# Convolving two query parts at once, and moving staged q and k by DMA, in a fused attention and gated-convolution kernel

## Chip, cores and metric

The kernel runs on one core of one Trainium2 chip. The metric is the device time of one execution in microseconds. A profile is one execution, taken separately; its span (214.9 us before) runs from the first to the last instruction and is some 1.7 us shorter than the time of that same execution. Executions whose time is more than 1.5% above the fastest of the same kernel count as slow and enter no comparison.

## The reference

```python
scores = np.matmul(q, k.transpose(0, 1, 3, 2)) / np.sqrt(D)        # B=4, H=8, S=768, D=64
mask   = window of +-1 block of 32 | first and last block, row and column | 3 sampled blocks per row block
attn   = softmax(np.where(mask, scores, -1e9))
x      = (attn @ v).transpose(0, 2, 1, 3).reshape(B, S, H * D)     # 4 x 768 x 512

h = np.maximum(x @ w_in, 0.0)                                      # 4 x 768 x 1024
for k in range(3):                                                 # 3 taps along the sequence
    conv_out += conv_w[k] * hp[:, k:k + S, :]                      # hp: h padded by one row on each side
out = (h / (1 + np.exp(-conv_out))) @ w_out                        # 4 x 768 x 512
```

## The kernel before

The words used below:

- A **pair** P (0 to 15) is two heads of one batch, four pairs to a batch. From pair 6 on its q and k are loaded, transposed by DMA into a **staging tile** `tmp`, and copied from there into a **slot** (TensorE transposes the first six pairs): tile `et` (first head) and tile `ot` (second), whose last 24 rows carry the mask.
- A **half** n (0 to 7) is one query part of 384 rows of one batch, g = n mod 2. It is 18 **units**; a unit is eight score blocks (TensorE, into one of two `st` tiles), one exponential of 128 x 1024 (ScalarE, `pt<-st`) and eight value products (`av<-vt,pt`). I speak of the first to the eighth half and of batches 0 to 3.
- The **layers** of a half follow its attention: eight groups of first-layer products (`mix<-xT,winb`), a relu each (`hE<-mix`, on ScalarE or VectorE), then four **convolution steps** of two 128-channel chunks (multiplies `m<-hE,cw`, additions `m<-m`, tanh, tanh+1, gate `gT`), then three second-layer blocks (`mix<-woutb,gT`).
- The **planner**, part of the kernel, orders all instructions of all engines from modelled durations and latencies. The order is fixed when the program is built. Each engine, and each DMA queue, then works strictly in that order and waits where an input is late.

The staging, in the form of before: two transposes in the sync queue, two copies by VectorE.

```python
NSLOT = 6                                        # slots for q/k of a pair; two staging tiles
t0 = op({"SP": 1.3}, xp(0), ..., alloc=tb, lat=TLAT)                   # tmp <- q by DMA transpose
t1 = op({"SP": 1.3}, xp(1), ..., lat=TLAT)                             # tmp <- k
ce = op({"DVE": 0.5}, put(ET, 0),  due, [t0, t1, ...], alloc=slot_b[P], uses=[tb])
co = op({"DVE": 0.5}, put(OT, 64), due, [ce], uses=[slot_b[P], tb])
# put: copy_to(e, t[s][0:64], tmp_t[tb.index][r0:r0 + 64])
```

The convolution of one half, one step:

```python
hE_t = many(3, [128, NFFC, 640], BF16, "hE");  gT_t = many(4, [128, NFFC, 384], BF16, "gT")   # one half each
m_t  = many(3, [128, 2, 768], BF16, "m");      tn_t = many(3, [128, 768], BF16, "tn")
def mul(x, slot):                                 # tap x: two chunks of 384 columns
    for (o0, o1, src, w) in muls(x):
        nc.vector.tensor_scalar(out=m_t[cb.index][:, slot, o0:o1], in0=src, scalar1=w, scalar2=None, op0=ALU.mult)
m1 = op({"DVE": tm}, mul(1, 0), ...)              # centre tap
m0 = op({"DVE": tm}, mul(0, 1), ..., [edge])      # after GpSimd has copied the edge columns
ad1 = op({"DVE": t_d2(768)}, add, ...);  m2 = op(...mul(2, 1)...);  ad2 = op(...add...)
th = op({"ACT": 0.745}, ...Tanh, scale=0.5...)    # sigmoid(z) = (1 + tanh(z/2)) / 2
g1 = op(...tanh + 1...);  gate = op(...gT = (tanh + 1) * h / 2...)
# ... [cut: the one row that the two parts of a batch share is mended by p1, p2, p3]
```

The softmax here doesn't subtract the row's maximum and nothing guards it: scores larger than these inputs give would overflow.

Of the kernel before, what the change touches and what calls it, by code (L numbers as in the profile page):

```python
# [11 lines left out]
ALU = mybir.AluOpType  # L12
# [36 lines left out]
FLEX = 0.0345  # L49
# [4 lines left out]
class Scheduler:  # L54
# [108 lines left out]
    def backward(self, order):  # L163
# [34 lines left out]
        for o, t in zip(order, end):  # L198
            o.prio = -t
            o.outs = []  # L200
            for b in o.allocs:
                b.index = None
                b.pool.holders = []
# [10 lines left out]
def kernel(  # L214
# [21 lines left out]
    NSLOT = 6  # L236
# [22 lines left out]
    NTMP, NVN, NNAT, NPT, NXK, NXT, NHE, NCV, NGT, NOS = 2, 3, 3, 5, 3, 4, 3, 3, 4, 4  # L259
# [7 lines left out]
    hE_t = many(NHE, [128, NFFC, 640], BF16, "hE")  # L267
    m_t = many(NCV, [128, 2, 768], BF16, "m")
    tn_t = many(NCV, [128, 768], BF16, "tn")
    gT_t = many(NGT, [128, NFFC, 384], BF16, "gT")  # L270
# [48 lines left out]
    T0, PACE0, PACE1 = 8.0, 0.91, 1  # L319
    OFF = 32.0894  # L320
    XLAT, TLAT = 3.908, 9.2201
    S_FIRST, A_FIRST, R_FIRST, N_FIRST = 5.6663, -4, 0.1178, 0.842
    F1S, F2A, F2S = 0.03, 2.344, 0.191
    WO = 22.9467
    OFFL = 28
    PE_ = 0.0
    PASSES = 12
# [116 lines left out]
    def rows_to(dst, src):  # L444
        return lambda e: nc.sync.dma_start(out=dst[64:88], in_=src[64:88])

# [9 lines left out]
    for s in range(1, NSLOT):  # L456
        for t, m in ((ET, e_mask), (OT, o_mask)):
            if s == 1 and t is OT:
                m[s] = op({"POOL": 1.8}, pool_copy(t[s][64:88], t[0][64:88]), 2.5, [m[0]])
            elif s == 1:  # L460
                m[s] = op({"DVE": 0.58}, rows_by(t[s], t[0]), T(4.5 * s) - 2.5, [m[0]])
            else:
                m[s] = op({"SP": 0.46}, rows_to(t[s], t[0]), T(4.5 * s) - 6, [m[0]], lat=6.0,
                          earliest=T(18 + 2 * s) if s > 3 else 0.0)
# [4 lines left out]
    for s in range(NHE):  # L469
        def z(e, s=s):  # L470
            nc.vector.memset(hE_t[s][:, :, 639:640], 0.0)
        he_z[s] = op({"DVE": 0.15}, z, T(2))
# [24 lines left out]
    def qk_loads(P):  # L497
# [9 lines left out]
        k_iss[P] = ik  # L507
        return nb, lq, lk
# [41 lines left out]
    for P in range(NP):  # L550
# [23 lines left out]
        else:  # L574
# [12 lines left out]
            t0 = op({"SP": 1.3}, xp(0), due - 8, [lq], alloc=tb, uses=[nb], lat=TLAT)  # L587
            t1 = op({"SP": 1.3}, xp(1), due - 8, [lk], uses=[nb, tb], lat=TLAT)
            ce = op({"DVE": 0.5}, put(ET, 0), due, [t0, t1, slot_first.get(P - 1)], alloc=slot_b[P], uses=[tb])
            co = op({"DVE": 0.5}, put(OT, 64), due, [ce], uses=[slot_b[P], tb])  # L590
# [29 lines left out]
    def norm_ops(n, hp):  # L620
# [33 lines left out]
        xtr[(n, hp)] = op({"SP": 1.25}, tr, due - 5, [nm], lat=XLAT, uses=[xk] + us, alloc=al)  # L654
# [91 lines left out]
    def conv_gate(due, edge, relus, muls, gate_out, gate_h, heb, gtb, first_gt, last_tap=None):  # L746

        cb = Buf(P_cv)

        def mul(x, slot):  # L750
            def fn(e):
                for (o0, o1, src, w) in muls(x):
                    nc.vector.tensor_scalar(out=m_t[cb.index][:, slot, o0:o1], in0=src, scalar1=w, scalar2=None,  # L753
                                            op0=ALU.mult)
            return fn

        def add(e):
            m = m_t[cb.index]
            nc.vector.tensor_tensor(out=m[:, 0], in0=m[:, 0], in1=m[:, 1], op=ALU.add)  # L759
        nmul = len(edge[1])  # L760
        tm = sum(t_d4s(w_) for w_ in edge[1])
        m1 = op({"DVE": tm}, mul(1, 0), due + 1.7, list(relus) + [cw_op], alloc=cb, uses=[heb])
        m0 = op({"DVE": tm}, mul(0, 1), due + 2, [edge[0]], uses=[cb, heb])
        ad1 = op({"DVE": t_d2(768)}, add, due + 2.2, [m1, m0], uses=[cb])
        m2 = op({"DVE": tm}, mul(2, 1), due + 2.1, [edge[0], ad1], uses=[cb, heb])
        ad2 = op({"DVE": t_d2(768)}, add, due + 2.3, [ad1, m2], uses=[cb])
        if last_tap is not None:
            last_tap(cb, ad2, due)
        th = op({"ACT": 0.745}, lambda e: nc.scalar.activation(  # L769
            out=tn_t[cb.index], in_=m_t[cb.index][:, 0], func=AF.Tanh, bias=0.0, scale=0.5),  # L770
            due + 2.8 - R_FIRST, [ad2], uses=[cb])
        g1 = op({"DVE": t_d4(768)}, lambda e: nc.vector.tensor_scalar(  # L772
            out=tn_t[cb.index], in0=tn_t[cb.index], scalar1=1.0, scalar2=None, op0=ALU.add),
            due + 3.6, [th], uses=[cb])

        def gate(e):
            o, h = gate_out(), gate_h()
            t = tn_t[cb.index]
            if len(h.shape) == 3:
                t = t.rearrange("p (a b) -> p a b", a=2)  # L780
            nc.vector.tensor_tensor(out=o, in0=t, in1=h, op=ALU.mult)  # L781
        return op({"DVE": t_d2(768)}, gate, due + 3.7, [g1], uses=[cb, heb] + ([] if first_gt else [gtb]),
                  alloc=gtb if first_gt else None)

    def out_block(n, c, due, deps, parts=None):

        gb = gt_buf[n]
# [5 lines left out]
        for (mb, acc, take, o0, o1, on, by) in parts:  # L793
            ob = Buf(P_os)
            prev = None
            for a in range(4):
                def fn(e, a=a, acc=acc, o0=o0, o1=o1):
                    for ffc in (2 * a, 2 * a + 1):
                        nc.tensor.matmul(out=acc()[:, 0:o1 - o0], lhsT=gT_t[gb.index][:, ffc, 128 * c:128 * c + 128],  # L799
# [10 lines left out]
    heb_n, cvl_b, cvl_op, gates_n = {}, {}, {}, {}  # L810
    for n in range(NHALF):
        b, g = divmod(n, 2)
        lastn = n == NHALF - 1
        heb, gtb = Buf(P_he), Buf(P_gt)
        heb_n[n], gt_buf[n] = heb, gtb
        if g == 0:
            cvl_b[n] = Buf(P_cvl)
        relus, gates = [], []
        base = T(18 * (n + 1)) + (OFFL if lastn else OFF)
        for ffc in range(NFFC):  # L820
            due = base + W * F1S * ffc
            relus.append(ffn1(n, ffc, due, lambda ffc=ffc, heb=heb: hE_t[heb.index][:, ffc, 128:512], heb, ffc == 0))
            if ffc % 2 == 0:
                continue
            f0 = ffc - 1

            def edges(e, f0=f0, heb=heb, g=g, n=n):
                h = hE_t[heb.index]
                nc.gpsimd.tensor_copy(out=h[:, f0:f0 + 2, 1:128], in_=h[:, f0:f0 + 2, 384:511])  # L829
                nc.gpsimd.tensor_copy(out=h[:, f0:f0 + 2, 512:639], in_=h[:, f0:f0 + 2, 129:256])  # L830
                if g == 1:
                    nc.gpsimd.tensor_copy(out=h[:, f0:f0 + 2, 0:1],
                                          in_=hE_t[heb_n[n - 1].index][:, f0:f0 + 2, 511:512])
                else:
                    nc.gpsimd.memset(h[:, f0:f0 + 2, 0:1], 0.0)
            ed = op({"POOL": 1.0}, edges, due + 1.5, relus[f0:f0 + 2], uses=[heb] + ([heb_n[n - 1]] if g else []))

            def muls(x, f0=f0, heb=heb):
                return [(384 * y, 384 * y + 384, hE_t[heb.index][:, f0 + y, 128 * x:128 * x + 384],
                         cw[:, x, f0 + y:f0 + y + 1]) for y in range(2)]  # L840

            def save(cb, ad2, due, f0=f0, n=n):
                al = cvl_b[n] if f0 == 0 else None
                cvl_op.setdefault(n, []).append(op({"POOL": 0.2}, lambda e: nc.gpsimd.tensor_copy(
# [83 lines left out]
```

## Time and profile before

| | before |
|---|---|
| time, median of 3 (range) | 214.94 us (214.78 to 215.05) |
| span of the profile | 214.9 us |
| TensorE, VectorE, ScalarE, GpSimd busy | 198.8, 189.7, 182.1, 81.8 us |
| first exponential of halves 1 to 8 | 8.2, 28.7, 47.9, 70.4, 92.1, 114.5, 138.2, 162.6 us |
| last normalisation ends | 187.6 us |

The prediction gives half starts 30.8, 51.0, 73.0, 94.5 and so on. They are wrong: each is the start of the third exponential of its half, two too late in the count. The stretches of the prediction (cut at 30.8, 117.0 and 187.6) are therefore not whole halves; its durations and its loads were taken over the same stretches, so its sums still hold together. But a whole half from the fifth on takes a mean of 23.9 us, not 23.3, so the room above TensorE's 22.5 us was 1.4, not 0.8.

Where I give TensorE's **load** below, it is not busy time but the sum of the measured spacings (scores 55 ns per 128 columns, value products 29, first layer 162, second 216) over the matmuls of a stretch. Length minus load is what TensorE **lost**.

### The profile page before, as it was taken

To read this page: it belongs to the slowest core of one execution; us is meant where nothing else is said; L and a number is where in the kernel's file an instruction comes from. 1 tells how busy PE (TensorE), PEld (TensorE's weight loads), DVE (VectorE), ACT (ScalarE), POOL (GpSimd) and SP (SyncE) were. 2 spreads that over 40 slices of the span, in tenths; PEclk is the share of its full clock that TensorE was granted. 3 is DMA by queue.
4 is the path that set the end of the run, shared out by engine and by line. 5 is a ranking of instruction groups with operands and counts; after the bars stand their busy time and mean duration, and the time that the engine had idled before them with its cause. 6 is when DMAs were issued, how large, how long until landed. Compare 5 with 4: busy or idle time off the path is not lost.

```text
span 214.9 us, 6588 instructions
## 1 busy us (share of the span) xinstructions
PE 198.8 (92%) x2579; PEld 150.4 (70%) x2596; DVE 189.7 (88%) x541; ACT 182.1 (85%) x227; POOL 81.8 (38%) x174
## 2 busy tenths in 40 slices
PE   7996999997999979999989999989999999998992
PEld 4785878886677857788768667667786787554441
DVE  6865627999989999479999999999999999999972
ACT  4595999999989989999998799989999999674541
POOL 8993414625505540446375302431241012443300
PEclk9999999999999999999999999999999999999999
DMA  6999994999999997899996993001110230022223
GB/s 170 152 177 204 199 203 61 142 154 134 190 136 212 150 119 80 148 146 213 168 136 106 129 204 107 18 20 62 59 23 21 71 116 21 18 98 101 99 98 146
DMA packets 50520, 25.84 MB, mean 120 GB/s; under 512 B 36321, under 2 KB 47353, under 8 KB 50489
## 3 DMA queue, kind: packets, MB, share of 16 engines
q0 software_dynamic: 18464, 11.14, 43.7%
q1 hardware_dynamic: 31592, 13.75, 31.6%
q10 hardware_dynamic: 432, 0.52, 0.7%
q8 instruction: 20, 0.33, 0.6%
q14 instruction: 12, 0.09, 0.2%
HBM read 23.08 MB, written 6.29 MB: 137 GB/s over the span
## 4 chain that ended last, share of the span: by engine, by line
DVE 59%; PE 15%; DMA 10%; ACT 6%; issue 5%; POOL 2%; SPq 1%; ACTq 0%; DVEq 0%; POOLq 0%
DVE m L753 19%; DVE m L759 10%; DVE hE L742 7%; PE st L678 6%; ACT pt L685 5%; DVE gT L781 5%; DVE xtok L631 5%; DMA nat<-in_k_dram 4%; DMA tmp<-nat 4%; PE mix L799 4%; DVE tn L772 3%; PE av L705 2%; DMA o2s<-in_q_dram 2%; DVE o2s L424 2%; PE st L799 2%
## 5 line engine op out<-in xcount | busy, mean ns | idle before, releaser
L685 ACT ACTIVATE pt<-st 128x1024 bf16<-128x1024 f32 x144 | 141.8, 1039 | 8.5 <-PE st L678 7.2
L705 PE MATMUL av<-vt,pt 128*128 128x65 bf16 x1152 | 57.9, 193 | 1.9 <-DVE vt L519 1.4
L753 DVE TENSOR_SCALAR m<-hE,cw 128x384 bf16<-128x384 bf16 x192 | 56.9, 346 | 0.2
L705 PEld LDWEIGHTS <-pt 128*128 128x128 bf16 x1152 | 50.4, 97 | 6.2 <-issue 1.7
L729 PE MATMUL mix<-xT,winb 128*128 128x384 bf16 x240 | 48.1, 325 | 1.9 <-DVE hE L742 1.1
L829 POOL COPY hE<-hE 128x254 bf16<-128x254 bf16 x32 | 18.4, 575 | 74.7 <-DVE hE L742 51.0
L799 PE MATMUL mix<-woutb,gT 128*128 128x512 bf16 x151 | 41.0, 379 | 2.4 <-DVE gT L781 1.6
L678 PE MATMUL st<-ot 88*128 88x128 bf16 (+1 forms) x224 | 42.5, 234 | 0.5 <-ACT pt L685 0.2
L678 PE MATMUL st<-et,ot 88*128 88x128 bf16 (+1 forms) x224 | 42.5, 234 | 0.1
L678 PE MATMUL st<-et 88*128 88x128 bf16 (+1 forms) x208 | 40.7, 239 | 1.7 <-ACT pt L685 1.7
L678 PEld LDWEIGHTS <-ot 88*128 88x128 bf16 x448 | 34.5, 97 | 10.1 <-issue 0.9
L678 PE MATMUL st<-ot,et 88*128 88x128 bf16 (+1 forms) x208 | 40.7, 239 | 0.7 <-ACT pt L685 0.4
L678 PEld LDWEIGHTS <-et 88*128 88x128 bf16 x416 | 32.3, 97 | 9.9 <-issue 3.3
L759 DVE TENSOR_TENSOR m<-m 128x768 bf16<-128x768 bf16 x64 | 35.1, 554 | 0.1
L769 ACT ACTIVATE tn<-m 128x768 bf16<-128x768 bf16 x32 | 27.7, 866 | 5.5 <-DVE m L759 5.4
L729 PEld LDWEIGHTS <-winb 128*128 128x128 bf16 x256 | 22.1, 97 | 13.1 <-issue 2.7
L799 PEld LDWEIGHTS <-gT 128*128 128x128 bf16 x200 | 16.5, 98 | 15.5 <-DVE gT L781 3.1
L742 DVE TENSOR_SCALAR hE<-mix 128x384 bf16<-128x384 f32 x37 | 20.2, 548 | 3.9 <-PE mix L729 3.8
L781 DVE TENSOR_TENSOR gT<-tn,hE 128x768 bf16<-128x768 bf16 x32 | 17.9, 562 | 0.1
L631 DVE TENSOR_TENSOR xtok<-av,rcp 128x384 bf16<-128x384 f32 x32 | 17.6, 549 | 0.3
L492 POOL DMA_DIRECT2D vn<-in_v_dram x16 | 11.9, 743 | 10.4 <-DVE vt L519 8.7
L830 POOL COPY hE<-hE 128x254 bf16<-128x254 bf16 x32 | 15.3, 479 | 0.0
(76 smaller groups left out, 168.7 us busy)
## 6 DMA issues: line engine op xcount, KB each, us to landing
out_dram<-o2s SPq DMA_DIRECT2D x23, 256.0 KB, 2.2
vn<-in_v_dram POOLq DMA_DIRECT2D x16, 192.0 KB, 6.2
nat<-in_q_dram POOLq DMA_DIRECT2D x15, 192.0 KB, 7.3
nat<-in_k_dram POOLq DMA_DIRECT2D x15, 192.0 KB, 6.4
winb<-in_moe_w_in_dram POOLq DMA_DIRECT2D x2, 512.0 KB, 12.2
woutb<-in_moe_w_out_dram POOLq DMA_DIRECT2D x2, 512.0 KB, 9.5
xT<-xtok SPq DMA_TRANSPOSE x27, 8.8
o2s<-in_k_dram ACTq DMA_DIRECT2D x2, 192.0 KB
```

The source lines that it names most:

```text
L631: nm = op({"DVE": 0.475}, lambda e: nc.vector.tensor_tensor(out=xtok_t[xk.index].rearrange("p c h d -> p h c d"), in0=o_of()[:, :, :, 0:64 ...
L678: nc.tensor.matmul(out=st_t[stb.index][:, 128 * x:128 * (x + n_)], lhsT=QK[kc % 2][s][0:88, 1, hh, kc // 2, :], rhs=QK[par][s][0:88, 0, hh ...
L685: e_op = op({"ACT": t_act(1024)}, lambda e, stb=stb, ptb=ptb: nc.scalar.activation(out=pt_t[ptb.index], in_=st_t[stb.index], func=AF.Exp, ...
L705: nc.tensor.matmul(out=av_t[av_buf[(n, P % 4)].index][:, off:off + 65], lhsT=pt_t[ptb.index][:, 128 * x:128 * x + 128], rhs=VT[P % NSLOT][ ...
L729: nc.tensor.matmul(out=tiles[hb.index][:, 0:384], lhsT=winb[:, fc, 128 * ffc:128 * ffc + 128], rhs=xT_t[xt_buf[n].index][:, fc, :], start= ...
L742: nc.vector.tensor_scalar(out=dst, in0=src, scalar1=0.5, scalar2=0.0, op0=ALU.mult, op1=ALU.max)
L753: nc.vector.tensor_scalar(out=m_t[cb.index][:, slot, o0:o1], in0=src, scalar1=w, scalar2=None, op0=ALU.mult)
L759: nc.vector.tensor_tensor(out=m[:, 0], in0=m[:, 0], in1=m[:, 1], op=ALU.add)
L769: th = op({"ACT": 0.745}, lambda e: nc.scalar.activation(out=tn_t[cb.index], in_=m_t[cb.index][:, 0], func=AF.Tanh, bias=0.0, scale=0.5), ...
L781: nc.vector.tensor_tensor(out=o, in0=t, in1=h, op=ALU.mult)
L799: nc.tensor.matmul(out=acc()[:, 0:o1 - o0], lhsT=gT_t[gb.index][:, ffc, 128 * c:128 * c + 128], rhs=woutb[:, ffc, o0:o1], start=(ffc == 0) ...
L829: nc.gpsimd.tensor_copy(out=h[:, f0:f0 + 2, 1:128], in_=h[:, f0:f0 + 2, 384:511])
```

## The change

The intent is to relieve VectorE. Batches 1 and 2 are convolved on both query parts at once ("wide": half as many instructions of twice the width). The 16 copies of pairs 8 to 15 from staging to slot become DMAs. The sixth slot goes (e4 shows that memory would still have held it), and h and gate tiles hold a batch instead of a half. The constants of the planner are new as well, and its choice between ScalarE and VectorE (`FLEX`) is off.

```diff
-FLEX = 0.0345
+FLEX = 0
-    NSLOT = 6
+    NSLOT = 5
+    WIDE = (1, 2)
+    PDMA = 8
-    hE_t = many(NHE, [128, NFFC, 640], BF16, "hE")      # NHE 3, NCV 3, NGT 4
-    m_t = many(NCV, [128, 2, 768], BF16, "m")
-    tn_t = many(NCV, [128, 768], BF16, "tn")
-    gT_t = many(NGT, [128, NFFC, 384], BF16, "gT")
+    hE_t = many(NHE, [128, NFFC, 2, 640], BF16, "hE")   # NHE 2, NCV 2, NGT 2
+    m_t = many(NCV, [128, 2, 1536], BF16, "m")
+    gT_t = many(NGT, [128, NFFC, 2, 384], BF16, "gT")
-    OFF, XLAT, TLAT = 32.0894, 3.908, 9.2201            # [cut: all planner constants]
+    OFF, XLAT, TLAT, PLAT, XE = 7.44, 3.5, 4.12, 4.0, 2.0
+            if P < PDMA:
                 ce = op({"DVE": 0.5}, put(ET, 0), due, [t0, t1, slot_first.get(P - 1)], alloc=slot_b[P], uses=[tb])
                 co = op({"DVE": 0.5}, put(OT, 64), due, [ce], uses=[slot_b[P], tb])
+            else:
+                ce = op({"SP": 0.46}, put_dma(ET, 0), due - 3, [t0, t1, slot_first.get(P - 1)], alloc=slot_b[P],
+                        uses=[tb], lat=PLAT)
+                co = op({"SP": 0.46}, put_dma(OT, 64), due - 3, [ce], uses=[slot_b[P], tb], lat=PLAT)
 # convolution step: gs = [0, 1] if wide else [g]; nothing is issued for g == 0 of a wide batch
-                for (o0, o1, src, w) in muls(x):
-                    nc.vector.tensor_scalar(out=m_t[cb.index][:, slot, o0:o1], in0=src, ...)
+                for y in range(2):
+                    nc.vector.tensor_scalar(out=split(m_of(slot))[:, y],
+                        in0=hE_t[hb.index][:, f0 + y, sl, 128 * x:128 * x + 384], ...)
+            srcs = relus[f0:f0 + 2] + (relu_n[n - 1][f0:f0 + 2] if both else [])     # waits for both parts' relus
+            if wide:
+                todo = [(m, c, gates_n[n]) for m in (n - 1, n) for c in range(3)] if g else []
 # [cut: mask rows of slots 2 and up by VectorE instead of DMA; edges; last tap only for narrow batches]
```

## The prediction

> **What bounds the kernel now.** I read the busy line of the page first, then the busy time of each engine in stretches cut at the first exponential of each half-batch (a half is 18 exponentials; their starts in the timeline are 8.2, 30.8, 51.0, 73.0, 94.5, 117.0, 141.1 and 165.0 us; the last normalisation ends at 187.6), then the groups by shape, then the waits, and last the timeline, to see how closely instructions follow one another.
>
> ```profile
> PE 198.8 (92%) x2579; PEld 150.4 (70%) x2596; DVE 189.7 (88%) x541; ACT 182.1 (85%) x227; POOL 81.8 (38%) x174
> ```
>
> Three engines lie within 17 us of each other, so none is the bound by its total alone. By stretch (PE, PEld, DVE, ACT, POOL busy):
>
> ```profile
> 73.00:94.00 21.00, 19.24 (x287) 15.33 (x288) 16.62 (x48) 19.70 (x24) 6.58 (x14) 1.00 0.91 111
> 94.00:117.00 23.00, 22.22 (x313) 17.64 (x312) 22.81 (x60) 21.68 (x28) 13.00 (x30) 1.00 1.23 165
> 117.00:141.00 24.00, 22.93 (x313) 17.49 (x314) 23.77 (x70) 22.17 (x29) 7.31 (x17) 1.00 0.64 108
> 141.00:165.00 24.00, 23.15 (x308) 17.56 (x309) 23.90 (x74) 23.16 (x32) 6.07 (x18) 1.00 0.14 41
> 165.00:188.00 23.00, 22.48 (x288) 16.53 (x290) 22.78 (x68) 20.73 (x27) 4.36 (x14) 1.00 0.17 53
> 188.00:215.00 27.00, 21.76 (x112) 10.78 (x112) 21.20 (x62) 12.24 (x22) 6.03 (x14) 0.99 0.28 108
> ```
>
> From 94 to 188 us VectorE is busy 93.3 of 94 us: it never rests, and the chain that ended last is 59% VectorE. That is what the change attacks. But the neighbours are nearly full too, and the question is how much room they leave. The groups:
>
> ```profile
> L753 DVE TENSOR_SCALAR m<-hE,cw 128x384 bf16<-128x384 bf16 x192 | 56.9, 346 | 0.2
> L759 DVE TENSOR_TENSOR m<-m 128x768 bf16<-128x768 bf16 x64 | 35.1, 554 | 0.1
> L424 DVE COPY ot<-tmp 64x1536 bf16<-64x1536 bf16 x10 | 5.8, 580 | 0.3
> L424 DVE COPY et<-tmp 64x1536 bf16<-64x1536 bf16 x10 | 5.7, 574 | 0.0
> ```
>
> These durations overlap (192 times 346 ns is 66 us, the union is 56.9), so I cost an instruction by the distance from its start to the next start where the engine was not idle between them. VectorE medians: convolution multiply 229 ns (mean 265, being stretched while GpSimd works), add 469, tanh+1 269, gate 469, relu 467, normalise 468 + 112, v copy 268, staging copy 469, output copy 601. ScalarE: exponential 904, tanh 734, relu 371. TensorE from the timeline:
>
> ```profile
> 150.43 0.41 PE L705 MATMUL av<-vt,pt 128*128 128x65 bf16 x8
> 150.67 0.22 PE L678 MATMUL st<-ot,et 88*128 88x128 bf16 x1
> ...
> 151.35 1.47 PE L729 MATMUL mix<-xT,winb 128*128 128x384 bf16 x8
> ```
>
> Eight value matmuls take 0.24 us, 0.030 each; eight first-layer matmuls 1.31 us (the next start is 152.66), 0.16 each. Scores step by 55 ns per 128 columns, the second layer by 216 ns.
>
> **Load of one steady half.** TensorE: 18 units of 8 score blocks (0.44) and 8 value matmuls (0.23) = 12.1; first layer 32 x 0.162 = 5.2; second layer 24 x 0.216 = 5.2; sum 22.5 us. ScalarE: 18 x 0.904 = 16.3, 4 tanh 2.9, relus and output copies about 1.7; sum 21. VectorE: 24 multiplies at 0.265 = 6.4, 8 adds 3.8, tanh+1 1.1, gate 1.9, about five relus 2.3, four normalisations 2.3, v 0.5, four staging copies 1.9, output 0.8; sum 21. The four halves from 94.5 us took 22.5, 24.1, 23.9 and 22.6. So VectorE is full, but TensorE needs 22.5 of a mean 23.3 itself. That is my main reading: a saturated engine with a second one right below it.
>
> **What the Trainium skill says.** "Perfetto Trace Analysis", section Identifying the Most-Contended Engine: occupancy is a fair measure for Vector and Scalar, matmul busy time is not; hence the spacing above. The trace agrees: 1152 value matmuls are recorded at a mean of 193 ns and follow each other every 29 ns. "VectorE: DVE Perf Modes", section The perf-mode tier table: bf16 copies and scalar operations in SBUF go four elements a cycle, two-tensor operations two; its errata section adds a fixed cost per instruction. The trace agrees: bf16 copies of 768 and 1536 columns take 268 and 469 ns, 201 ns for 768 more columns (3.8 per ns, four at 0.96 GHz), thus 67 fixed. "Perfetto Trace Analysis", section Optimizing Scalar/DVE Operations, says that GpSimd and VectorE share an SBUF port; the multiply's mean of 265 against its median of 229 agrees. "DMA: Bandwidth & Descriptors", section Anatomy of one DMA, puts a fixed cost of about 2 us on a DMA; here the transposes into the staging tile land after 6.5 us and the output stores after 2.2.
>
> **The change part by part.**
> 1. Batches 1 and 2 convolve both halves at once: 96 multiplies of 384 columns become 48 of 768. Doubling costs 384/3.84 = 100 ns more, so 96 x 0.229 = 22.0 becomes 48 x 0.329 = 15.8: -6.2 us. 32 adds become 16, each 768/1.92 = 400 ns longer: 15.0 to 13.9, -1.1. Sixteen tanh+1 become 8: -0.6. Sixteen gates become 8: -0.6. The edge fix-up of these two batches goes (two of four): -0.6. ScalarE's 16 tanh become 8 of 1536 columns: about 11.7 to 11.0, -0.7. GpSimd copies the same edge columns in half as many instructions.
> 2. q and k of pairs 8 to 15 go from staging to slot by DMA: 16 copies x 0.469 = -7.5 us of VectorE, at the price of 16 DMAs of 196 KB in the sync queue, mostly after 60 us.
> 3. The mask rows of slots 2 and up are copied by VectorE instead of eight DMAs: six copies more, about 0.77 each, +4.6 us, all before about 35 us, where VectorE is idle a third of the time.
> 4. The built order also shows three relus net and two output copies leaving VectorE (-2.6), the relus and copies going to ScalarE (+2).
>
> VectorE: -6.2 -1.1 -0.6 -0.6 -0.6 -7.5 -2.6 +4.6 = about -14.6 us net, some -19 in its saturated stretch. ScalarE is level within 1 us. TensorE has the same 2596 matmuls: nothing.
>
> **What of it reaches the end.** TensorE's work summed by spacing is 192.6 us in both kernels: scores 63.1, values 33.4, first layer 41.5, second 41.5, transposes 4.9, warm-up 7.2, rest 1. So 22 us of the 214.9 are not TensorE work, and only these can be won. After the last normalisation both built orders hold 24.0 us of TensorE work (the last half's first layer, 5.2, and eleven output blocks); with 3.4 us from the last matmul to the end that is 27.4, and 27.3 was measured: **the tail cannot shrink**. The rest by stretch, TensorE's load counted from the built orders:
> - To 30.8 us, set by loads and latencies: eight mask DMAs fewer, my guess is -0.8: 30.0.
> - 30.8 to 117.0, 86.2 us: load 79.5 before, 77.2 after (2.3 us shift later, since a wide convolution waits for both halves). Stalls were 6.7 us; with VectorE at about 64 us of load they should fall, I take 4.8: 82.0.
> - 117.0 to 187.6, 70.6 us: load 65.1 before, 67.1 after. Stalls 5.5, I take 3.4: 70.5.
> - Tail 27.3.
> Sum 209.8 us, 2.4% faster: of 19 us taken from the full engine I expect about five at the end.
>
> **Rivals.**
> (a) VectorE is the true bound and the time falls by most of the 19 us, to 198-202. For: 99% busy for 94 us. Against: TensorE alone would need to be 98% dense from its first real work. I give it little.
> (b) TensorE and ScalarE bind at once and nothing comes of it: 212-215. For: score tiles have two buffers, so exponential and scores hold each other, and in the after-order some halves are as heavy on ScalarE as on TensorE (sixth half: 24.1 and 23.5 us); two convolution buffers instead of three. Against: the waits view shows only 7.2 us of exponentials waiting for scores now.
> (c) The sync queue is in order: a staging copy waiting for its slot holds the transposes behind it, and with five slots and two staging tiles pairs arrive late, above 216. For: the transposes already take 6.5 us to land. Against: a slot is free 18 units, about 22 us, before a pair of batches 2 and 3 is needed, twice the 6.5 + 4 us of the path, and the DMA share falls to 0.14 after 141 us.
>
> **Range and chances.** 209.8 lies between (a) and (b), nearer (b); each stall term is uncertain by 2 us and the start by 1, so 204.5 to 214.0. The 2% line is 210.6, just above my number: faster 0.55, same 0.41, slower 0.04.
>
> **What would show it.** Right: VectorE's busy time about 175 us, with idle time waiting for TensorE from 94 us on; wide multiplies spaced near 330 ns and wide adds near 870; TensorE denser than 95% from 94 to 188; a tail of 27 us after the last normalisation. Wrong: wide multiplies at 430 ns or more (the fast mode lost over two strips); VectorE still 99% busy; exponentials waiting for a staged pair (c); or a tail shorter than 26 us, which would mean that the second layer started earlier than I count.

## More of the kernel before

The prediction shows the main lines. Here are the fifth to the eighth half of before with the right cuts, in the view of engines by stretch. The columns are the stretch, its length, then busy microseconds (and instructions) of TensorE, its weight loads, VectorE, ScalarE and GpSimd, then the granted TensorE clock, the DMA share and GB/s.

```profile
core 0: us, PE busy (x) PEld busy (x) DVE busy (x) ACT busy (x) POOL busy (x), PEclk, DMA share, GB/s
92.10:114.50 22.40, 21.68 (x312) 17.29 (x311) 21.80 (x59) 21.08 (x27) 11.94 (x28) 1.00 1.33 170
114.50:138.20 23.70, 23.09 (x311) 17.47 (x311) 23.41 (x68) 22.41 (x30) 7.70 (x16) 1.00 0.65 111
138.20:162.60 24.40, 23.07 (x314) 17.73 (x314) 24.34 (x73) 23.02 (x30) 7.57 (x22) 1.00 0.14 41
162.60:187.60 25.00, 24.45 (x316) 17.92 (x317) 24.75 (x75) 23.12 (x30) 4.36 (x14) 1.00 0.17 52
```

Read the third busy figure against the length: VectorE is full in every one of these halves. Then read the first and the fourth: TensorE and ScalarE are close below it, in every one of them too. The work is even from half to half.

## The result

| | before | after |
|---|---|---|
| time, median of 4 on the same chip (range) | 215.0 us (214.78 to 215.53) | 221.41 us (220.5 to 221.83) |
| span of the profile | 214.9 | 219.4 |
| VectorE busy, instructions | 189.7, 541 | 175.7, 442 |
| lengths of halves 1 to 8, and the tail | 20.5 19.2 22.5 21.6 22.4 23.7 24.4 24.9, 27.3 | 20.0 20.2 20.7 21.8 25.6 26.5 20.6 28.3, 27.4 |

The kernel after is 2.9% slower: ratio 1.0289, 95% interval 1.0249 to 1.0329. A ratio here is the mean time of one kernel's fast runs over that of the other's in the same rounds, so it is not quite the ratio of the medians quoted.

The busy line of the page after:

```profile
PE 199.3 (91%) x2581; PEld 150.5 (69%) x2596; DVE 175.7 (80%) x442; ACT 183.6 (84%) x221; POOL 78.0 (36%) x146
```

VectorE did lose its 14 us. The same view by stretch as above, for halves 5 to 8 of after, shows where it lost them:

```profile
91.10:116.60 25.50, 20.34 (x295) 16.05 (x295) 9.96 (x23) 19.41 (x23) 5.27 (x9) 1.00 1.04 173
116.60:143.10 26.50, 24.80 (x322) 18.67 (x321) 26.33 (x53) 24.77 (x28) 9.66 (x16) 1.00 0.80 132
143.10:163.70 20.60, 20.43 (x302) 16.40 (x301) 14.43 (x31) 19.98 (x23) 6.22 (x12) 1.00 0.28 75
163.70:192.00 28.30, 27.56 (x330) 19.43 (x332) 28.30 (x67) 25.81 (x31) 7.83 (x18) 1.00 0.19 56
```

VectorE is busy for 10.0 of 25.5 us, then for 26.3 of 26.5, then for 14.4 of 20.6, then for 28.3 of 28.3. Its sum over the four halves fell by 15.3 us (94.3 to 79.0), and the four halves together grew by 5.4. The saving became idleness in the odd halves; the even ones are as full as before, and longer.

TensorE's loss rose from 25.1 us to 29.4 over the span, by 4.3, which accounts for the 4.5 us that the span grew. The fifth half alone adds 4.6: 6.1 us against 1.5. Waits of after in that half (engine, line, what it waited for: total us, times, longest):

```profile
POOL nat L493 <- DMA tmp<-nat: 9.1, 2, 8.4
DVE rcp L639 <- PE av L715: 8.1, 2, 5.8
...
ACT pt L695 <- PE st L688: 5.6, 3, 3.2
...
PE st L688 <- DMA ot<-tmp: 5.1, 2, 2.9
```

Scores wait twice for a query half that a copy DMA has not landed yet, and exponentials wait for those scores. The chain that ended last, in the same half (start, us, what), says how the lateness arose:

```profile
93.41 0.39 SPq L591
...
93.86 1.27 SPq L662
...
95.23 1.53 SPq L584
...
96.80 5.96 DMA ot<-tmp
...
102.81 0.49 PE st L688 x5
```

L584 issues the transposes into staging, L591 the copies, L662 the transposes of the normalised output, all in one in-order queue (SPq). The copy landed 5.96 us after the chain left the queue, and the scores started 0.1 us later. A copy by VectorE took 0.5 to 0.6 us. The copies' medians from issue to landing, from the page after:

```profile
et<-tmp SPq DMA_DIRECT2D x8, 192.0 KB, 4.5
ot<-tmp SPq DMA_DIRECT2D x8, 192.0 KB, 3.5
```

In after, pair 11's first transpose was issued at 91.63 us, just when pair 9's copy, issued at 84.61, had landed (91.56): a DMA copy also holds its staging tile until it lands.

**The profile of before hides a part of the loss.** The execution that it shows took 216.58 us, 1.6 above the median. In it a load of k (`nat<-in_k_dram`, issued at 11.3 us) took 9.0 us to land. The same load took 7.0 us in e2 and 6.0 in e9 (below), which keep the order of before, and there the first half ended at 26.7 and 26.3 us instead of 28.7. In the six traces with the order of after it ended at 27.7 to 28.7. So the profiles show 4.5 of the 6.4 us by which the time grew, and about 2 us lie in the first half. No run tests which part of the change they come from; e6, which has neither wide convolutions nor DMA copies, also ends its first half at 28.1 and makes it up later.

In the groups by shape, the instructions themselves are as costed (mean ns of one is the last number before the idle time):

```profile
L771 DVE TENSOR_SCALAR m<-hE,cw 128x384 bf16<-128x384 bf16 x96 | 28.0, 341 | 0.4
L771 DVE TENSOR_SCALAR m<-hE,cw 128x768 bf16<-128x768 bf16 x48 | 21.5, 486 | 0.3
...
L777 DVE TENSOR_TENSOR m<-m 128x1536 bf16<-128x1536 bf16 x16 | 15.7, 982 | 0.1
```

From start to start, where no GpSimd copy runs beside it, a wide multiply takes 329 ns and a wide addition 866: the fast mode is not lost over two strips.

### The profile page after: what moved, and what is told of

It is laid out like the page before. It is cut to its first block, busy times and chain, and to the rows that moved or that the text cites. A ratio compares the mean times of both kernels' runs of the same rounds, so it can differ in the third digit from the quotient of the medians.

```text
span 219.4 us, 6478 instructions
## 1 busy us (share of the span) xinstructions
PE 199.3 (91%) x2581; PEld 150.5 (69%) x2596; DVE 175.7 (80%) x442; ACT 183.6 (84%) x221; POOL 78.0 (36%) x146
## 4 chain that ended last, share of the span: by engine, by line
PE 48%; DVE 29%; ACT 11%; issue 5%; DMA 4%; SPq 2%; DVEq 0%; ACTq 0%
PE st L688 15%; PE mix L739 11%; ACT pt L695 9%; PE mix L809 8%; DVE m L771 8%; PE av L715 8%; DVE m L777 5%; DMA ot<-tmp 4%; PE st L809 2%; DVE hE L752 2%; PE av L375 2%; DVE gT L790 2%; DVE ot L542 2%; DVE xtok L641 2%; DVE et L542 2%
## 5 line engine op out<-in xcount | busy, mean ns | idle before, releaser
L715 PE MATMUL av<-vt,pt 128*128 128x65 bf16 x1152 | 57.2, 193 | 1.6 <-DVE vt L522 1.5
L771 DVE TENSOR_SCALAR m<-hE,cw 128x384 bf16<-128x384 bf16 (+1 forms) x144 | 49.4, 389 | 0.6
L777 DVE TENSOR_TENSOR m<-m 128x768 bf16<-128x768 bf16 (+1 forms) x48 | 33.0, 694 | 0.2
L847 POOL COPY hE<-hE 128x254 bf16<-128x254 bf16 x32 | 15.6, 515 | 44.8 <-DVE hE L752 20.6
L845 POOL COPY hE<-hE 128x508 bf16<-128x508 bf16 x16 | 12.8, 827 | 48.8 <-ACT hE L750 27.6
L752 DVE TENSOR_SCALAR hE<-mix 128x384 bf16<-128x384 f32 x33 | 18.0, 549 | 14.8 <-PE mix L739 14.7
L786 ACT ACTIVATE m<-m 128x768 bf16<-128x768 bf16 (+1 forms) x24 | 25.8, 1074 | 4.5 <-DVE m L777 4.3
L809 PEld LDWEIGHTS <-gT 128*128 128x128 bf16 x200 | 17.3, 98 | 15.9 <-DVE gT L790 1.8
L493 POOL DMA_DIRECT2D nat<-in_q_dram x15 | 12.2, 813 | 14.2 <-DMA tmp<-nat 8.4
L790 DVE TENSOR_TENSOR gT<-m,hE 128x768 bf16<-128x768 bf16 (+1 forms) x24 | 16.5, 689 | 0.1
```

The costliest lines, as they stand in the source:

```text
L715: nc.tensor.matmul(out=av_t[av_buf[(n, P % 4)].index][:, off:off + 65], lhsT=pt_t[ptb.index][:, 128 * x:128 * x + 128], rhs=VT[P % NSLOT][ ...
L752: nc.vector.tensor_scalar(out=dst, in0=src, scalar1=0.5, scalar2=0.0, op0=ALU.mult, op1=ALU.max)
L771: nc.vector.tensor_scalar(out=split(m_of(slot))[:, y], in0=hE_t[hb.index][:, f0 + y, sl, 128 * x:128 * x + 384], scalar1=cw[:, x, f0 + y:f ...
L777: nc.vector.tensor_tensor(out=m_of(0), in0=m_of(0), in1=m_of(1), op=ALU.add)
L786: th = op({"ACT": t_act(w) + 0.055}, lambda e: nc.scalar.activation(out=m_of(1), in_=m_of(0), func=AF.Tanh, bias=0.0, scale=0.5), due + 2. ...
L790: return op({"DVE": t_d2(w)}, lambda e: nc.vector.tensor_tensor(out=gT_t[gb.index][:, f0:f0 + 2, sl], in0=split(m_of(1)), in1=hE_t[hb.inde ...
```

## The experiments

Eighteen kernels were run, each beside the kernel before on the same chip. "Frozen order" means that the edit sits inside the function that emits an instruction, so the planner's order stays; "replanned" means that the planner saw the edit. All outputs were correct except where said. The 2 by 2 of the middle group is the backbone; the last two groups test the cause.

### The copies alone, order frozen

**e1: the kernel after, its sixteen copies by VectorE.**

```diff
-  nc.sync.dma_start(out=t[s][0:64], in_=tmp_t[tb.index][r0:r0 + 64])
+  nc.vector.tensor_copy(out=t[s][0:64], in_=tmp_t[tb.index][r0:r0 + 64])
```

> The changed kernel with its planned order kept instruction for instruction, only the 16 staging copies of pairs 8 to 15 are written by VectorE (about 0.47 us each, 7.5 us in all) instead of by DMA. Theory Q (the pairs come late because the copies stand in the in-order sync queue and take 3.5 to 6 us to land; TensorE waited 5.1 us for them): the waits of TensorE on staged pairs vanish, the half from 91 us shrinks from 25.5 to about 22.5 us, total 214 to 217 us. Theory W (the wide convolution starves VectorE from 91 to 117 us, 10.3 of 26 us busy, and then floods it, 26.0 of 26): stays at 219 to 222 us, VectorE still below half busy in that stretch and full in the next.

Measured: 222.12 us (220.97 to 222.67), ratio 1.0314 (1.0269 to 1.0359). No gain: taking the DMA wait away changes nothing in sum. Its fifth and sixth half by stretch:

```profile
92.00:113.60 21.60, 20.29 (x295) 16.23 (x297) 13.82 (x30) 19.37 (x23) 4.54 (x8) 1.00 1.00 142
113.60:143.10 29.50, 25.37 (x324) 18.73 (x323) 29.20 (x58) 25.07 (x29) 10.06 (x16) 1.00 0.56 80
```

The fifth half fell from 25.6 to 21.6 us, as it should without the wait (VectorE was 64% busy in it, not below half as theory W had it). The sixth rose from 26.5 to 29.5, with VectorE busy for 29.2 of it: the copies it got back (and a fourth half of 23.4 instead of 21.8) took up what was won. My reading was that the loss has two causes in after, and each hides the other; e17 and e18 below test it.

**e2: the kernel before, its copies of pairs 8 to 15 by DMA.**

```diff
+  if P >= 8: nc.sync.dma_start(out=t[s][0:64], in_=tmp_t[tb.index][r0:r0 + 64])
   else: copy_to(e, t[s][0:64], tmp_t[tb.index][r0:r0 + 64])
```

> The kernel before with its planned order kept, only the 16 copies of pairs 8 to 15 out of the staging tile are DMAs on the sync queue. VectorE loses 7.5 us of work while it is full. Theory Q: the pairs come late here too, 217 to 221 us, with TensorE waiting for staged pairs. Theory W: no harm in the DMAs as such, 211 to 215 us.

Measured: 224.04 us (222.73 to 225.25), ratio 1.0409 (1.0354 to 1.0464). Here the DMA copies cost 9 us, more than theory Q had said. From the waits over the whole span of e2, and its fifth half by stretch:

```profile
PE st L680 <- DMA et<-tmp: 7.0, 1, 7.0
```

```profile
91.00:122.50 31.50, 23.78 (x308) 18.46 (x305) 20.23 (x57) 21.59 (x28) 11.99 (x31) 0.84 0.96 156
```

One pair, pair 10, comes 7 us late. Its transposes were issued at 85.67 and 87.61 us and had landed by 93.25, but its copies were issued at 100.89 and 102.29 and landed by 107.42. Ahead of them in the queue stood pair 11's transposes, which waited until 94.1 us for pair 9's DMA copies to land and free the staging tile; those transposes, two stores and two transposes of the normalised output then took 6.7 us to issue, almost without a gap. The granted clock fell to 0.50 from 103 to 111 us, in and after the stall (0.84 on average over this stretch), which adds to the cost. With VectorE idle for a third of the stretch, that engine was not the bound.

**e9: the kernel before, the same copies by GpSimd.**

```diff
-  return lambda e, s=s, tb=tb: copy_to(e, t[s][0:64], tmp_t[tb.index][r0:r0 + 64])
+  if P >= 8: nc.gpsimd.tensor_copy(out=t[s][0:64], in_=tmp_t[tb.index][r0:r0 + 64])   # else as before
```

> The kernel before, planned order kept, the copies of pairs 8 to 15 out of the staging tile as GpSimd copies (no DMA, no landing; GpSimd is 62% idle). In the second run the same copies as DMAs cost 9 us. Theory Q (it is the landing of about 5 us, the place in the sync queue and the staging tile held meanwhile that hurt, not that the order was made for VectorE): 211 to 216 us, no wait of TensorE for a staged pair. If any other engine than the planned one spoils the order: 219 us and more.

Measured: 234.89 us (234.22 to 235.61), ratio 1.092 (1.0886 to 1.0954). A miss. From the groups on GpSimd and the waits of e9:

```profile
L587 POOL COPY ot<-tmp 64x1536 bf16<-64x1536 bf16 x8 | 12.7, 1590 | 0.5
```

```profile
ACT tn L771 <- DVE m L761: 16.6, 12, 4.3
```

A copy takes 1.5 to 1.6 us there. Tanh waits for VectorE's additions 16.6 us in total. My reading is that the edge columns come late behind the copies in GpSimd's order and the convolution with them; no run separates that from the stretching of VectorE's multiplies that the last section measures.

### Wide or narrow, VectorE or DMA copies, replanned

All four keep the five slots, tiles and planner constants of after.

**e3: narrow everywhere, DMA copies** (`WIDE = ()`).

> The changed kernel without wide convolutions (all four batches half by half), staging copies still by DMA, five slots; the order is planned anew. Theory Q: pairs still come late, 218 to 222 us. Theory W: VectorE no longer alternates between idle and full, 211 to 215 us.

Measured: 218.9 us median (218.59 to 220.85, without the slow run of 230.22), ratio 1.0197 (1.0136 to 1.0259). Its profile fell in the slow run and is not read.

**e5: wide, VectorE copies** (`PDMA = 16`).

> The changed kernel with all staging copies on VectorE and the order planned anew for that (in the first run only the engine was swapped inside the old order). Theory Q alone: 213 to 216 us. Theory W (unevenness of the wide convolution is a cost of its own, about as large as what the queue costs): 218 to 222 us, VectorE full for 25 us and more in the half from about 115 us while below 60% in the half before it.

Measured: 221.48 us (221.14 to 223.32), ratio 1.0329 (1.0282 to 1.0375). In this order the sixth half takes 24.9 us (VectorE never rests) and the eighth 32.3 (VectorE busy 32.2), so where the loss falls depends on the order.

**e6: narrow, VectorE copies** (`WIDE = ()`, `PDMA = 16`).

> The changed kernel with neither wide convolutions nor DMA copies (five slots, two convolution buffers, mask rows on VectorE and the new planning constants remain), planned anew. Theory Q plus W: with both causes gone 213 to 217 us. A third theory P (the new planning constants, with transposes believed to land after 4.1 us, give a worse order whatever the parts): 218 to 222 us.

Measured: 214.69 us (214.62 to 215.33), ratio 1.0004 (0.9978 to 1.0031). So the fifth slot, the batch-wide tiles, the mask rows on VectorE and the new constants cost nothing together. The four corners:

| | VectorE copies | DMA copies |
|---|---|---|
| narrow | 214.7 (e6) | 218.9 (e3) |
| wide | 221.5 (e5) | 221.4 (after) |

Either part alone loses: DMA copies 4.2 us, the wide convolution 6.8. Together they lose 6.7, not 11.0. (The corners ran on different chips; by the ratios it is 4.1, 7.0 and 6.1.) The sixth half shows the difference between e6 and a wide kernel. First e6, halves 5 and 6:

```profile
92.50:115.20 22.70, 21.85 (x296) 16.86 (x298) 22.52 (x62) 21.39 (x27) 11.69 (x22) 1.00 0.95 147
115.20:138.20 23.00, 22.82 (x320) 17.88 (x322) 22.84 (x67) 22.19 (x29) 7.76 (x18) 1.00 0.62 103
```

VectorE is full here as well, but never starved first, and TensorE is full beside it.

**e10: e3 with three staging tiles** (`NTMP = 3`).

> The changed kernel without wide convolutions (218.9 us with its DMA copies, 214.7 with VectorE copies), with three staging tiles instead of two, DMA copies, planned anew. If the harm is that a copy by DMA holds one of two staging tiles for 3.5 to 6 us so that the next pair's transposes start late: 214 to 216 us. If it is the landing time and the queue themselves: 217 to 220 us.

Measured: 218.73 us (217.59 to 219.61), ratio 1.0164 (1.0118 to 1.0211). A third tile wins nothing over e3, so a shortage of staging tiles is an unlikely reason for the 4 us of DMA copies (the planner's order changed as well, and after and e2 do show transposes waiting for a staging tile, so it is not excluded).

**e11 and e12: only one batch wide, VectorE copies** (`WIDE = (1,)` and `WIDE = (2,)`, `PDMA = 16`).

> The changed kernel, staging copies on VectorE, only batch 1 convolved on both halves at once. Theory W, in the form that unevenness costs wherever it stands: about half of the 6.8 us that both batches cost, 217 to 219 us. In the form that batch 1's late work fits into the idle time that follows, and only batch 2's collides with batch 3: 214 to 216 us.

> The same with only batch 2 convolved on both halves at once. Unevenness anywhere: 217 to 219 us. Collision with batch 3's convolution in the last half of attention: 219 to 223 us, with VectorE full through 28 us and more before the last normalisation.

Measured: e11 222.42 us, ratio 1.0351 (1.0294 to 1.0407); e12 215.55 us (215.35 to 215.79), ratio 1.0021 (1.0002 to 1.004). Batch 1 alone costs the whole 7 us, batch 2 at most 1. Both lie outside every range that I had expected. By stretch, e11's fifth and sixth half:

```profile
93.20:114.50 21.30, 20.25 (x294) 16.19 (x296) 14.32 (x32) 18.51 (x20) 5.81 (x12) 1.00 0.76 123
114.50:140.30 25.80, 21.57 (x302) 16.21 (x302) 25.67 (x52) 23.97 (x27) 7.35 (x13) 1.00 0.75 103
```

and e12's seventh and eighth:

```profile
136.20:157.80 21.60, 21.50 (x322) 17.38 (x321) 13.52 (x30) 20.66 (x26) 6.01 (x12) 1.00 0.11 28
157.80:186.40 28.60, 27.30 (x323) 19.17 (x323) 28.60 (x67) 26.19 (x32) 9.71 (x18) 1.00 0.18 52
```

In both, VectorE idles for 7 to 8 us and then has a half in which it never rests. What differs is TensorE in the full half: in e12 it is busy for 27.3 of 28.6 us, in e11 for 21.6 of 25.8. By spacing, layer products make up 14.5 us of TensorE's load there in e12 and 6.6 in e11; what e11 did not do then turns up after the last normalisation (23.3 us of layer work in its tail, 18.2 in e6's). TensorE starved in the middle and was overworked at the end. This contrast is read from traces; no run tests why batch 2 had enough queued. It also says that idling first and being full afterwards is not enough for a loss: e12 does it and is only 0.2% slower than before.

### Planner and slots

**e4: the kernel after with six slots** (`NSLOT = 6`), **e8: wide, VectorE copies, six slots, planner constants and `FLEX` of before.**

> The changed kernel with six slots instead of five (it fits in memory), order planned anew. If the missing slot is what makes the pairs late: 214 to 217 us and no wait of TensorE for staged pairs. Theory Q (queue and landing time, not slots) and theory W: 219 to 222 us.

> Wide convolutions of batches 1 and 2, but six slots, staging copies on VectorE and the planning constants of the kernel before. Theory W: slower than before by 2 us and more, 217 to 222 us, with VectorE alternating between idle and full. Theory P: the wide convolution gains what its work saves, 211 to 214 us.

Measured: e4 228.19 us (227.02 to 230.39, without a slow run of 231.15), ratio 1.0619 (1.0539 to 1.0699); e8 226.1 us (225.83 to 226.27), ratio 1.0525 (1.0504 to 1.0546). Both are slower than any range that I had expected. Neither run points to the lost slot or the new constants as the cause: with the slot back, or with both back, the wide kernel is slower still. Both were replanned, so they also differ in order, and why they are slower than after stays open.

**e7: the kernel after planned with longer DMA latencies** (`TLAT` 7.2 and `XE` for all pairs, `PLAT` 6.0).

> The changed kernel, planned with the landing times that the trace shows at the busy time: 9.2 us instead of 4.1 (6.1 for the first eight pairs) from issue to landing of a staging transpose, 6 instead of 4 us of a staging copy. Theory P and theory Q: the plan issues transposes and copies earlier or puts other work before the late pairs, 214 to 218 us. Theory W: still 219 us and more.

Measured: 238.6 us (237.14 to 239.13), ratio 1.1097 (1.1056 to 1.1139). A clear miss. Latencies nearer to the measured ones gave a far worse order: its fifth half, from 94.4 us, took 36.8. A planner's constants are tuned parameters, not measurements; changing three of them moves everything.

### Is it the wait for late gates?

At this point I held theory G: a wide gate comes late and in a lump, and second-layer products in TensorE's fixed order wait for it with the scores behind them. The rival V: VectorE itself is full in that half, and everything it owes the others is late. Four kernels with frozen order take the gates of batches 1 and 2 out of the second layer; the output is wrong (relative error 17).

```diff
-  lhsT=gT_t[gb.index][:, ffc, g, 128 * c:128 * c + 128]
+  lhsT=woutb[:, ffc, 128 * c:128 * c + 128] if b in (1, 2) else gT_t[gb.index][:, ffc, g, 128 * c:128 * c + 128]
```

**e13, on e11.**

> The kernel with batch 1 alone wide and all staging copies on VectorE (222.4 us), same instructions in the same order on every engine, but the second layer of batches 1 and 2 takes its stationary matrix from the output weights (resident since early) and not from the gate tile. The output is wrong on purpose; the matrix engine then never waits for a gate of these two batches. Theory G (batch 1's wide convolution costs 7 us because second-layer products stand in the matrix engine's fixed order ahead of scores and wait for late, coarse gates): it falls by 5 to 7 us, to 215.5-217.5, and the sixth half (25.7 us from 114.5) falls to about 20-21. Theory V (the exponentials are late because VectorE itself is full in that half: relus, normalisations and the value copies that it owes the others stand behind 866-ns additions; gates matter no more than these): it falls by less than 2 us, to 220.5-222.

**e14, on e6.**

> Control of the run before: the same removal of the gate wait in the narrow kernel with staging copies on VectorE (214.7 us). Theory G: narrow gates come in time, so at most 2 us are won, 213-214.7. Theory V: the same size of gain as in the wide kernel, under 2 us. If this one gains as much as the wide one (both 4 us or more), waiting for gates is a general cost of the schedule and not what the wide convolution added.

**e15, on e1.**

> The kernel after in its own order with VectorE doing the sixteen staging copies (222.1 us; its sixth half from 113.6 took 29.4 us), second layer of batches 1 and 2 freed from the gates. Theory G: down by 6 to 8 us, to 214-216, the sixth half to about 22. Theory V: 220 or more, the sixth half at 27 or more.

**e16, on the kernel after.**

> The kernel after itself (221.4 us) with the second layer of batches 1 and 2 freed from the gates. Here the fifth half (25.6 us) waits for staged query rows by DMA, and the sixth (26.5) is full of first- and second-layer work. Theory G with the DMA as a second cause that overlaps it: the fifth half stays at 25-26, and 0 to 3 us are won: 218.5-221.4. If it falls to 216 or lower, the wait for staged rows is not a cause in its own right. Theory V: 220.5-221.5.

| | with gates | second layer freed |
|---|---|---|
| e13, from e11 | 222.42 | 223.87 (223.62 to 224.48) |
| e14, from e6 | 214.69 | 214.43 (214.21 to 215.35) |
| e15, from e1 | 222.12 | 222.88 (221.44 to 224.07) |
| e16, from after | 221.41 | 221.76 (221.67 to 222.6, without a slow run of 226.77) |

Nothing is won anywhere beyond the noise: by the ratio e14 gains 1.2 us on e6, but its interval reaches 1.0017. Theory G falls. The timeline of ScalarE in e13's sixth half shows another way in which VectorE's lateness reaches the scores (start, us, instruction, and in brackets the idle time before it and its releaser):

```profile
123.16 1.48 ACT L786 ACTIVATE m<-m 128x1536 bf16<-128x1536 bf16 x1 [0.36 <-DVE m L777]
124.55 1.92 ACT L695 ACTIVATE pt<-st 128x1024 bf16<-128x1024 f32 x2
...
129.83 1.48 ACT L786 ACTIVATE m<-m 128x1536 bf16<-128x1536 bf16 x1 [1.05 <-DVE m L777]
131.22 3.74 ACT L695 ACTIVATE pt<-st 128x1024 bf16<-128x1024 f32 x4
```

A wide tanh stands in ScalarE's order ahead of the exponentials, waits for VectorE's last addition, and then takes 1.48 us itself. With two score tiles, the scores wait for those exponentials. It is one way among several (relus that hold a `mix` tile are another), and all of them start at VectorE.

### Is it VectorE's load in the sixth half?

The last two kernels shed that load without touching order or count. Two of the three taps of batch 1, and both additions, are cut to 8 columns; ScalarE's tanh stay whole. The result is wrong, but lay within the tolerance of the output check, which thus does not see these taps.

```diff
+        cut = 8 if hb is he_buf.get(1) else 768 * len(gs)        # hb of batch 1
+            n_ = 384 if x == 1 else min(cut, 384)
-  out=split(m_of(slot))[:, y], in0=hE_t[hb.index][:, f0 + y, sl, 128 * x:128 * x + 384], ...
+  out=split(m_of(slot))[:, y, :, 0:n_], in0=hE_t[hb.index][:, f0 + y, sl, 128 * x:128 * x + n_], ...
-  nc.vector.tensor_tensor(out=m_of(0), in0=m_of(0), in1=m_of(1), op=ALU.add)
+  nc.vector.tensor_tensor(out=m_of(0)[:, 0:cut], in0=m_of(0)[:, 0:cut], in1=m_of(1)[:, 0:cut], op=ALU.add)
```

**e17, on e1 (VectorE copies).**

> The kernel after in its own order with VectorE doing the sixteen staging copies (222.1 us, sixth half 29.4 us with VectorE busy 29.1 of it), and two of the three taps of batch 1's convolution cut to 8 columns (both additions too): some 10 us of VectorE's work leave the sixth half, the instructions and their order stay, ScalarE's tanh stay whole. The output is wrong on purpose. Theory V (VectorE's bunched convolution bounds that half): the sixth half falls to 23.5-25.5, where ScalarE's own 25.0 us of work stop it, and the time falls by 4 to 6 us, to 216-218. Theory N (neither gates nor VectorE's load; the order itself holds the scores): less than 1.5 us, 220.5-222.

Measured: 216.62 us (216.26 to 216.94), ratio 1.0097 (1.0064 to 1.0131): 5.5 us less than e1 (on another chip; 4.7 by the two ratios). The sixth half, by stretch:

```profile
114.50:139.00 24.50, 24.39 (x324) 18.54 (x323) 21.18 (x55) 24.28 (x28) 9.00 (x16) 1.00 0.61 100
```

**e18, on the kernel after (DMA copies).**

> The same cut in the kernel after itself, whose sixteen copies go by DMA (221.4 us; fifth half 25.6 us with 5.1 us of waiting for staged rows, sixth half 26.5). Theory D+V (two causes in the same order, each enough for most of the loss): the fifth half stays at 25-26, the sixth falls from 26.5 to 24-25, and the time is 218.5-221, 2 us or more above the run without the DMA copies. Theory V alone (the wait for staged rows costs nothing of its own): it falls to the same 216-218 as that run. Theory N: 220.5-222.

Measured: 218.92 us (217.66 to 219.69), ratio 1.0202 (1.0145 to 1.0259): 2.5 us less than after (1.9 by the two ratios, whose intervals just touch). Fifth and sixth half:

```profile
91.10:116.20 25.10, 21.97 (x295) 17.05 (x296) 8.72 (x24) 19.40 (x23) 4.54 (x9) 0.93 1.03 172
116.20:140.70 24.50, 24.39 (x324) 18.56 (x323) 19.44 (x50) 24.28 (x28) 8.38 (x16) 1.00 0.92 143
```

Both fell where theory V (with the DMA wait as a second cause) put them. In both, the sixth half ends at 24.5 us, where TensorE (24.4 busy) and ScalarE (24.3) stop it. The fifth half of e18 stays at 25.1 us against 21.5 in e17, although VectorE has nothing to do there: that is the wait for staged rows, and 2.3 us between the two times are its net cost. The granted clock averaged 0.93 in that half of e18, against 1.00 in e17's, which is a part of the difference. It is not all of 3.6 because the fourth half is shorter with the DMA copies (21.8 against 23.3).

**What the runs add up to.** In after's own order, 221.4 us becomes 218.9 without batch 1's bunched load, and 216.6 without the DMA copies too. The remaining 2.0 us to before (214.6 in those rounds) were not taken apart by a run; the traces put about as much into the first half (28.7 us in e17, 26.7 and 26.3 in e2 and e9). The eighth half, batch 2's full one, is still 28.2 us in both, but the seventh makes up for it (20.6; before 24.4 and 24.9). One control is missing: the same cut in the narrow e6. Its sixth half, with TensorE busy for 22.8 of 23.0 us, seems to leave little to win, but no run shows it; so e17 shows that VectorE's load holds that half, and that bunching is what made it so rests on e6 and e11. No version here beats both kernels: e6 equals before within 0.3%, and e14, at 0.9948 (0.988 to 1.0017), is no valid kernel.

## Why the prediction was wrong

**Costs of the instructions: right.** Wide multiply 329 ns (costed 329), wide addition 866 (869), VectorE busy 175.7 us (about 175). The tail was 27.4 us (27.3).

**TensorE's load by stretch: right in size.** With the right cuts, halves 2 to 5 hold 77.4 us of load before and 75.7 after, halves 6 to 8 hold 66.9 and 69.5. The prediction saw the same shift of some 2 us, and gave its reason ("since a wide convolution waits for both halves").

**The stall terms: the step that failed.** The prediction says of the first middle stretch: "Stalls were 6.7 us; with VectorE at about 64 us of load they should fall, I take 4.8", and of the second: "Stalls 5.5, I take 3.4". By whole halves they were 8.4 and 6.2 before. After, they are 12.6 and 5.9: up 4.2 in the first stretch where a fall of 1.9 was taken, down 0.3 in the second where 2.1 was taken. These two terms are 8 us of the roughly 10 us between forecast and result in the span. The rest is TensorE's shifted load, by the right cuts 0.9 us net where I had -0.3.

**Why they failed.** The first term failed in the fifth half, where TensorE lost 6.1 us (before 1.5) and scores waited for staged rows: that is rival (c), below. The second failed because VectorE's load is bunched: with batch 1's load cut (e18) that stretch lost 3.7 us, near the 3.4 that I had taken. I spread VectorE's load over an 86-us stretch and compared sums, 64 against 86. The engine does not work on a sum. A wide step can start only when the relus of both query parts exist, so a batch's convolution, which before lay in two halves, comes in one: 17.3 us of it in the sixth half by spacing, after 2.8 in the fifth (before: 13.0 and 10.7). The runs show the consequence: shedding the load of that half wins 5.5 us where no DMA waits lie ahead of it (e17 against e1). The two also trade places: without the DMA copies TensorE lost 1.8 us in the fifth half and 5.8 in the sixth (e1), with them 6.1 and 2.9 (after). I had written down the precondition and used it for TensorE's work only. What stays open is why e12 pays next to nothing for the same pattern.

**The start: missed, though it looks right.** The profiles have the first half ending 0.4 us earlier (guess 0.8), but only because the profiled execution of before was late there; against e2 and e9 it ends 1.0 to 2.4 us later. The prediction compared a sum of spans with a time, which happened to be the same number (214.9). A usual span of before is about 213.4 us (e9's rounds), so the miss in time, 221.4 against 209.8, is some 2 us larger than in the span.

**Rival (c): dismissed on a wrong comparison.** The sign that I named for it came true: scores waited 5.1 us for staged rows in the fifth half, and exponentials 5.6 us for scores. I had set it against 22 us of slack in slots. A sixth slot did not help (e4), and neither did a third staging tile (e10), though both were replanned. What came late was the issue: transposes, copies and output transposes share one queue, so a copy also waits for whatever the entries ahead of it wait for (in e2 another pair's transposes, and these for a staging tile), and lands 3.5 to 4.5 us later (6.0 in the chain shown, 7.4 at most) where VectorE took 0.5. The figure of 4 us for the landing was right; that the wait ahead of it comes on top was missing. In e2 that made 9 us, in e3 against e6 4.2, in the order of after 2.3.

**Rival (b)** named the right suspicion, two engines right below VectorE and two convolution buffers, and the remark that the sixth half would be heavy on ScalarE and TensorE (24.1 and 23.5 us) is just where e17 and e18 stop (24.5). But it was priced as "nothing comes of it", not as a loss.

**Additivity.** The parts were summed as if independent. Alone they cost 4.2 and 6.8 us, together 6.7: in after, the DMA copies take 16 copies off VectorE and shorten the fourth half (21.8 us against 23.4 in e1) and the full sixth (26.5 against 29.4) by about what they add to the fifth (25.6 against 21.6).

## What to carry to other kernels

When several engines are near full, count load and bound half by half, at the grain of the buffers that couple the engines, and not over the whole run: merging instructions saves work but makes the merged one wait for the later of its inputs, and a saturated engine that idles first has lost the saving (whether it also costs time depends on what the other engines have queued: e11 lost 7 us, e12 next to nothing). A copy moved off an engine onto an in-order DMA queue trades its duration for a landing time plus the waits of everything ahead of it in the queue. And two causes in series can hide each other, so an undo that wins nothing does not acquit the part that was undone.

## What the Trainium skill lacked or had wrong

- "SBUF — State Buffer", section SBUF: two separate sides, says that VectorE instructions in a two-port mode, or with two SBUF inputs against a reading GpSimd instruction, share a port pair with GpSimd as an exclusive lock for the whole instruction. Nothing wrong was found: the traces agree, but medians hide it. In before, a multiply of 384 columns takes a median of 229 ns from start to start with no GpSimd copy beside it (118 of them) and 370 with one over more than half of it (50); in after the wide one takes 329 and 626. For the additions of 768 columns in before the two medians are alike, 469 and 467, yet 3 of the 12 beside a copy took 556 to 672 ns, and none of the 46 others over 477; of the gates, 3 of 8 took 565 to 667. In after two wide additions beside copies took 1164 and 1165 ns, against a median of 866.
- "DMA: Bandwidth & Descriptors", section Anatomy of one DMA, gives about 2.0 us plus bytes over 436 KB per us, for DMAs that GpSimd issues. If the copies of 192 KB, which the sync queue issues, followed it, that would make an estimate of 2.5 us. Measured here: 4.5 and 3.5 us at the median (2.6 to 7.4; ten of the sixteen landings are recorded), beside other transfers on the same engines. No page was found with a time from issue to landing for the sync queue.
- The same section states that semaphore waits happen on the issuing sequencer; it draws no price for a queue shared by transfers with different waits. In e2 pair 10's copies were issued 7.6 us after their transposes had landed.
